# A fused attention and mixture-of-experts kernel: both halves of the small product "states times w1" put into one slot, the second half in banks of another PSUM pool

## The chip, the cores and the metric

The kernel runs as one program on one core of a Trainium2 chip. The metric is the device time of one execution in microseconds (us); lower is better. Six executions of the kernel before gave a median of 439.1 us, between 437.64 and 439.78.

The engines are named as the profile names them: PE (TensorE, the matrix engine; PEld is its loading of weights), DVE (VectorE), ACT (ScalarE), POOL (GpSimd) and SP (SyncE, which here only issues transfers). [...]

## What is computed

There are B = 8 batches with H = 8 heads, S = 512 tokens of D = 64 numbers per head, and 32 states per head. The reference, cut to what matters here:

```
scores  = scale * x @ state^T;  a  = softmax(scores)      # per batch and head
xread   = a @ state                                        # 512 rows
sread   = softmax(scale * state @ x^T) @ x                 # 32 rows
rows    = concat(xread, sread), heads side by side         # 4352 rows of 512
e       = argmax(rows @ w_gate);  g = softmax(...)[e]      # one of 8 experts for each row
out     = g * (relu(rows @ w1[e]) @ w2[e])                 # w1: 512 x 1024, w2: 1024 x 512
```

All of it is float32. The kernel uses that `xread @ w1` is `a @ (state @ w1)`: for each batch it first makes **G = states @ w1** (256 rows, that is 8 heads of 32 states, by 1024), a small product, and then multiplies the attention weights with G. G is what the change moves.

## The kernel before, in words

Each batch takes its most frequent expert. For batch b the work on PE is, in this order: G of the batch (`states_w1`, L585), the "up" product of attention weights and G with a relu (`up` L602 or `up_by_halves` L656), and the "down" product with w2 (`down` L709 or `down_by_halves` L734). Batches 0 and 1 use `down`; batches 2 to 7 use `down_by_halves`. G of batch b + 1 is made inside the down of batch b, so that the up of b + 1 can follow at once.

**`states_w1`** makes G in two halves of 512 columns. Each half takes two PSUM banks (tiles `pG`) and 8 matrix products that use only a 64 x 32 corner of the array each: 64 rows of states and 32 columns (`pg[g][ts(q, 32), :]`, q = 0..3, g = 0, 1), so the eight fill the array side by side. In the trace a float32 product is two passes, so a half is 16 instructions. The two banks of a half are then copied to the tile G by ACT.

**`down_by_halves`** computes the 512 x 1024 by 1024 x 512 product of a batch with seven half-size products in place of eight, each of 8 full-array products of 256 columns (16 passes in the trace). They stand in program order as pX, pD, pX (accumulated on the first), pY, pZ, pW, pD (accumulated). Between them lie sums: after the first pD, DVE updates the tile Sa and POOL updates the tile Ta, and both are operands of pY; after pY the same again, with Ta an operand of pW and Sa of the last pD. ACT scales pX into the rows of the result, DVE adds the other products to them, POOL issues the stores.

After product n (1 to 7) `done()` (L767) runs a **slot**: first the first part of `between_products(n)` (L1137), then one step of `slots` (`with_weights`, L1167), then the second part of `between_products(n)`. In the first part, before the change, n = 3 makes the first half of G and n = 4 the second, both in the banks of the pool `ps_t` (two banks). In the second part, n = 4 puts the four transfers of w1 for batch b + 2 on the list `lazy` (there is one w1 tile, so they wait for the last reader of the w1 before), and n = 5 lets POOL begin the sums of G and of the attention weights for the up of b + 1 (`up_sums`, L627).

A step of `slots` issues one transfer from `lazy` (SP) and then advances `work`, which from batch 2 on is **`rounds`** (L1019): three rounds for the rows of the states, sorted by expert, four experts at a time. A round transposes its rows (`ptx`), multiplies with w1 of its four experts (`pgh`, two pieces), transposes (`pth`) and multiplies with w2 (`pgy`, two pieces). A piece is 16 products, 32 passes in the trace, on a 128 x 32 part of the array each, four side by side. `rounds` yields between the pieces, so a piece falls into a slot every three to four slots: in the down of batch 3 into slot 2, of batch 4 into slot 1, of batch 5 into slot 5 (after the two `pth` of slot 4), of batch 6 into slot 3. In the down of batch 2 no piece falls into any slot. Each round's weights come through the tiles `s` (7 of 1 MB), loaded by SP from the list `need` as the pieces use them up.

The pool `ps_p` (four banks, tag "p") serves all products of up and down (`bank()`, L197); `ps_g` (two) serves the rounds and `ps_t` (two) serves G and, in batch 7, the two tiles `pE`. `evict` (L177) copies PSUM to SBUF and takes ACT and DVE in turn. The order on each engine is the order in which the program is written (`InOrder`, L40).

Of the kernel before, what the change touches and what calls it, by code (L numbers as in the profile page):

```python
# [9 lines left out]
FP32 = mybir.dt.float32  # L10
# [10 lines left out]
def kernel(  # L21
# [32 lines left out]
    pe, dve, act, gp, sp = (InOrder(e) for e in (nc.tensor, nc.vector, nc.scalar, nc.gpsimd, nc.sync))  # L54

    B, H, S, D = x.shape
# [109 lines left out]
    stG = const.tile([128, B, 4, NS], FP32)  # L166
# [27 lines left out]
    soft, rows_of = {}, {}  # L194
    G = hT = None

    def bank(name):  # L197
        return ps_p.tile([128, 512], FP32, tag="p", name=name)
# [36 lines left out]
    def turn_scores(pc, sx, i):  # L235

        dve.transpose(sx[:, i].rearrange("p b n -> p (b n)"), pc[:, i, 0:256])
# [9 lines left out]
    def exponential(sx, i):  # L247
        act.activation(sx[:, i], sx[:, i], AF.Exp, bias=0.0, scale=SCALE)
# [194 lines left out]
    def begin():  # L443

        nonlocal G, hT

# [28 lines left out]
        soft[0] = (sx,)  # L475
        G, hT = new_G(), new_hT()
        turn_scores(pc, sx, 0)
        less_max(sx, one, dve)
        exponential(sx, one)
        states_w1(G, w1s[0], stG[:, 0], (0,), cut=2)  # L480
        turn_scores(pc, sx, 1)
# [5 lines left out]
        near, far = range(NFC // 2), range(NFC // 2, NFC)  # L487
        up(G, aT[0], hT, one, fs=near)
        states_w1(G, w1s[0], stG[:, 0], (1,))
        turn_scores(pc, sx, 2)  # L490
        turn_scores(pc, sx, 3)
# [57 lines left out]
    def expert_of(table, i, engines=(SP,)):  # L549
        _, (e,) = nc.values_load_multi_w_load_instructions(  # L550
            table[0:1, i:i + 1], engines=list(engines), min_val=0, max_val=E - 1,
            skip_runtime_bounds_check_because="the table holds experts' numbers")
        return e

    w1s, w2s = {}, {}

    def w1_parts(b, e, cols=1):

        t = w1s[b] = wpool.tile([128, NDC, F], FP32, tag="w1", name="w1t")
        rows = moe_w1[ds(e, 1)].rearrange("o (c p) f -> p (o c) f", p=128)  # L560
        f = F // cols
        return [lambda k=k: sp.dma_start(out=t[:, :, ts(k, f)], in_=rows[:, :, ts(k, f)]) for k in range(cols)] if cols > 1 else \
            [lambda k=k: sp.dma_start(out=t[:, k], in_=rows[:, k]) for k in range(NDC)]

    def w2_parts(b, e):
        t = w2s[b] = wpool.tile([128, NFC, DM], FP32, tag="w2", bufs=2, name="w2t")
        rows = moe_w2[ds(e, 1)].rearrange("o (c p) f -> p (o c) f", p=128)
        return [lambda k=k: sp.dma_start(out=t[:, ts(k, 2)], in_=rows[:, ts(k, 2)]) for k in range(NFC // 2)]
# [13 lines left out]
    def new_G():  # L582
        return ffn.tile([128, 2, F], FP32, tag="G", name="G")

    def states_w1(G, w1t, st, halves=(0, 1), bank=bank, cut=1):  # L585

        for k in halves:
            pg = [bank("pG") for _ in range(2)]
            for q in range(4):
                for g in range(2):  # L590
                    pe.matmul(pg[g][ts(q, 32), :], lhsT=st[ts(g, 64), q, :],
                              rhs=w1t[ts(g, 64), q, ts(k, 512)], start=True, stop=True, skip_group_check=True)
            for c in range(cut):
                for g in range(2):
                    act.copy(G[:, g, ts(cut * k + c, 512 // cut)], pg[g][:, ts(c, 512 // cut)])
        return G

    def new_hT():

        return [ffn.tile([128, 2, S], FP32, tag="hT", bufs=NFC // 2, name="hT") for _ in range(NFC // 2)]  # L600

    def up(G, a, hT, i=ALL, insert=None, at=(1, 3, 5, 7), fs=range(NFC)):  # L602

        n = i.stop - i.start
        for f in fs:
            ph = bank("ph")[:, 0:128 * n]
            for g in range(2):
                pe.matmul(ph, lhsT=G[:, g, ts(f, 128)], rhs=a[:, i, g, :], start=(g == 0), stop=(g == 1))
            relu(hT[f // 2][:, f % 2].rearrange("p (c i t) -> p i c t", c=NC, i=4)[:, i],
                 ph.rearrange("p (i c t) -> p i c t", i=n, c=NC))  # L610
            if insert and f in at:
                next(insert, None)
        return hT
# [13 lines left out]
    def up_sums(G, a):  # L627

        Sx, Tx = new_sums("Sb"), new_sums("Tb")
        T3 = ffn.tile([128, 256], FP32, tag="T3", name="T3")  # L630
        S1, S2 = (Sx[:, ts(k, 2)].rearrange("p u t -> p (u t)") for k in range(2))
        S3 = Tx[:, 0:2].rearrange("p u t -> p (u t)")
        T1, T2, T3 = Tx[:, 2], Tx[:, 3], T3[:]

        def A(i, k):
            return G_block(G, i, k)

        def B(k, j):
            return a_block(a, k, j)

        def v(t):
            return t.rearrange("p (c i t) -> p c i t", c=2, i=4)

        gp.tensor_tensor(S1, A(1, 0), A(1, 1), ALU.add)
        gp.tensor_tensor(v(T1), B(0, 1), B(0, 0), ALU.subtract)
        gp.tensor_tensor(S2, S1, A(0, 0), ALU.subtract)
        gp.tensor_tensor(v(T2), B(1, 1), v(T1), ALU.subtract)
        gp.tensor_tensor(S3, A(0, 0), A(1, 0), ALU.subtract)
        gp.tensor_tensor(v(T3), B(1, 1), B(0, 1), ALU.subtract)

        def last():
            gp.tensor_tensor(v(T2), B(1, 0), v(T2), ALU.subtract)
            gp.tensor_tensor(S2, A(0, 1), S2, ALU.subtract)
        return S1, S2, S3, T1, T2, T3, last
# [54 lines left out]
    def down(hT, w2t, store, insert=None, between=None):  # L709
        for c in range(NC):  # L710
            py = bank("py")
            for f in range(NFC):
                pe.matmul(py[:], lhsT=hT[f // 2][:, f % 2, ts(c, 128)], rhs=w2t[:, f, :],
                          start=(f == 0), stop=(f == NFC - 1))
                if insert and f == 3:
                    next(insert, None)
            store(c, py)
            if insert:
                step = between(c)
                next(step)  # L720
                next(insert, None)
                next(step)
# [123 lines left out]
    def store_batch(b):  # L846
        rows = out[ds(b * SO, S)].rearrange("(p c) f -> p c f", c=NC)

        def store(c, py):
            y = ffn.tile([128, DM], FP32, tag="y", bufs=YB, name="y")  # L850
            act.activation(y[:], py[:], AF.Copy, scale=gw[:, NC * b + c, :])
            no_dep(act.dma_start(out=rows[:, c], in_=y[:]))
        return store
# [76 lines left out]
    late = {}  # L930
# [191 lines left out]
    def batch(b):  # L1122

        nonlocal G, hT

        def between(c):
            nonlocal G
            if c == 1 and b:
                G = states_w1(new_G(), w1s[b + 1], stG[:, b + 1])
            yield  # L1130
            if c == 2 and not b:
                G = states_w1(new_G(), w1s[b + 1], stG[:, b + 1])
            if c == 1 and 0 < b < B - 2:
                lazy.extend(w1_parts(b + 2, expert_of(eb, b + 2)))
            yield

        def between_products(n):  # L1137
            nonlocal G
            if n in (3, 4) and b + 1 < B:
                if n == 3:  # L1140
                    G = new_G()
                states_w1(G, w1s[b + 1], stG[:, b + 1], (n - 3,),
                          lambda name: late["ps_t"].tile([128, 512], FP32, tag="t", bufs=2, name=name))
            yield
            if n == 4 and b + 2 < B:
                lazy.extend(w1_parts(b + 2, expert_of(eb, b + 2)))
            if n == 5 and b + 1 < B:
                sums_of[b + 1] = up_sums(G, aT[b + 1])
            yield

        if b < NE:
            down(hT, w2s[b], store_batch(b), slots, between)
        else:
            last = down_by_halves(b, hT, w2s[b], slots, between_products)
        if 0 < b < B - 2:
            lazy.extend(w2_parts(b + 2, expert_of(eb, b + 2)))
        if b + 1 in sums_of:
            hT = up_by_halves(G, aT[b + 1], sums_of[b + 1], new_hT(), slots)
        elif b + 1 < B:
            hT = up(G, aT[b + 1], new_hT(), insert=slots, at=(1, 3, 5, 7) if b + 1 < NE else (1, 3, 4, 5, 6, 7))  # L1160
        if b == B - 1:
            return last
        if b == 0:
            e2 = expert_of(eb, 2)
            lazy.extend(w1_parts(2, e2) + w2_parts(2, e2))
# [12 lines left out]
    for b in range(B):  # L1178
        last = batch(b)
# [116 lines left out]
```

## Time and profile before

| what | value |
|---|---|
| median of 6 executions | 439.1 us (437.64 to 439.78) |
| the profiled execution | 438.35 us; its span, from first to last instruction, 434.3 us |
| PE busy | 426.1 us of the span (98%) |
| DVE, ACT, POOL busy | 220.3, 128.9 and 153.3 us |
| granted TensorE clock | 1.000 over the whole span |
| transfers | 110.04 MB, mean 253 GB/s |
| G in the downs of batches 2 to 6 | 10 halves of 1.02 us each in the chain of work that ended last |

The profile's page gives busy time of each engine, the span in 40 slices, the chain of work that ended last (followed back from the last instruction), and groups of instructions by operation and tile. The chain in order of time lists pieces as start, length and tile; lengths in it are from the start of one piece to the start of the next on the chain, so two pieces that differ by what precedes them differ in length. The timeline lists instructions by engine with the idle time before them. All operations are recorded through one helper, so every line is L48, and tiles tell them apart.

The downs with `down_by_halves` begin at 163.85 (batch 2), 206.88 (3), 253.98 (4), 304.42 (5), 351.48 (6) and 397.95 us (7).

### The profile page before, as it was taken

The numbers are of one execution on the slowest core, as the hardware profiler recorded it, in microseconds if no ns is written. First come the engines' busy times: TensorE is split into PE (matmuls) and PEld (weight loads), VectorE is DVE, ScalarE is ACT, GpSimd is POOL, SyncE is SP. The second block draws the span as 40 slices with busy tenths as digits, with TensorE's granted clock in tenths as the row PEclk, the third lists the DMA queues.
The fourth block names the chain that finished last, engine by engine and source line by source line (L and its number), as shares of the span: only waits on it lengthen the run. The fifth ranks groups of instructions, "written<-read, shape, count | busy, mean of one in ns | idle before, by whom it ended". The sixth has DMA issues, their size and how long they took to land.

```text
span 434.3 us, 10177 instructions
## 1 busy us (share of the span) xinstructions
PE 426.1 (98%) x3927; PEld 289.7 (67%) x3927; DVE 220.3 (51%) x473; ACT 128.9 (30%) x297; POOL 153.3 (35%) x143
## 2 busy tenths in 40 slices
PE   7899999999999999999999999999999999999996
PEld 7676555555545558686668667776867685768665
DVE  5668967587686547434424251624442370527142
ACT  1455134552451532213221241013240242015100
POOL 2010231233222512473327424634336253644231
PEclk9999999999999999999999999999999999999999
DMA  5991559653685454899999799689947998875312
GB/s 146 338 339 45 190 195 334 192 209 127 203 309 171 158 173 123 298 345 399 339 379 398 249 333 391 257 288 396 386 142 258 374 385 286 312 273 187 97 35 73
DMA packets 64513, 110.04 MB, mean 253 GB/s; under 512 B 12943, under 2 KB 22415, under 8 KB 64464
## 3 DMA queue, kind: packets, MB, share of 16 engines
q1 hardware_dynamic: 60240, 99.99, 67.1%
q0 software_dynamic: 2240, 7.08, 4.3%
q10 hardware_dynamic: 1984, 2.31, 1.5%
q8 instruction: 32, 0.52, 0.5%
q14 instruction: 17, 0.14, 0.1%
HBM read 94.15 MB, written 14.95 MB: 251 GB/s over the span
## 4 chain that ended last, share of the span: by engine, by line
PE 95%; DVE 2%; DMA 1%; ACT 0%; issue 0%; ACTq 0%; POOL 0%; DVEq 0%
PE ph L48 23%; PE py L48 13%; PE pX L48 10%; PE pD L48 8%; PE pY L48 5%; PE pZ L48 5%; PE pgh L48 5%; PE pgy L48 5%; PE pW L48 5%; PE pc L48 4%; PE pG L48 3%; PE pw L48 2%; PE pt L48 2%; PE pE L48 2%; DMA wg<-in_moe_w_gate_dram 1%; PE pl L48 1%
## 5 line engine op out<-in xcount | busy, mean ns | idle before, releaser
L48 PE MATMUL py<-w2t,hT 128*128 128x512 f32 x128 | 59.1, 604 | 0.0
L48 DVE TENSOR_TENSOR hT<-ph,hT 128x512 f32<-128x512 f32 x50 | 34.6, 692 | 40.7 <-PE ph L48 40.7
L48 POOL TENSOR_TENSOR Ta<-w2t,Ta 128x1024 f32<-128x1024 f32 x12 | 30.6, 2548 | 46.6 <-PE pY L48 19.9
L48 PE MATMUL pX<-w2t,hT 128*128 128x256 f32 x192 | 43.7, 381 | 0.0
L48 PEld LDWEIGHTS py<-w2t,hT 128*128 128x128 f32 x128 | 23.0, 189 | 26.3 <-issue 25.3
L48 PEld LDWEIGHTS pX<-w2t,hT 128*128 128x128 f32 x192 | 36.2, 190 | 6.4 <-issue 1.7
L48 ACT ACTIVATE hT<-ph 128x512 f32<-128x512 f32 (+2 forms) x50 | 22.7, 461 | 40.2 <-PE ph L48 40.2
L48 PE MATMUL ph<-aTl,G 128*128 128x256 f32 (+1 forms) x112 | 33.8, 444 | 0.0
L48 DVE SCALAR_TENSOR_TENSOR yh<-pY,gw,yh 128x256 f32<-128x256 f32 x22 | 9.2, 478 | 44.3 <-PE pY L48 37.7
L48 PE MATMUL ph<-aTe,G 128*128 128x128 f32 (+2 forms) x128 | 30.4, 388 | 0.6 <-DVE aTe L48 0.4
L48 ACT ACTIVATE yh<-pX,gw 128x256 f32<-128x256 f32 x34 | 13.7, 473 | 52.6 <-PE pX L48 52.6
L48 POOL DMA_DIRECT2D out_dram<-yh x23 | 16.8, 730 | 34.2 <-DVE yh L48 17.6
L48 ACT ACTIVATE hT<-hT 128x512 f32<-128x512 f32 x30 | 18.9, 630 | 30.7 <-DVE hT L48 30.7
L48 PEld LDWEIGHTS ph<-aTl,G 128*128 128x128 f32 x112 | 20.6, 190 | 9.6 <-issue 7.7
L48 POOL TENSOR_TENSOR sx<-sx,mx 128x1024 f32<-128x1024 f32 x6 | 11.5, 1913 | 38.5 <-DVE mx L48 38.5
L48 PEld LDWEIGHTS ph<-aTe,G 128*128 128x128 f32 x128 | 18.8, 191 | 9.3 <-issue 6.5
L48 ACT COPY G<-pG 128x512 f32<-128x512 f32 (+1 forms) x34 | 17.1, 568 | 24.3 <-PE pG L48 24.3
L48 PE MATMUL pY<-Ta,Sa 128*128 128x256 f32 x96 | 22.2, 384 | 0.0
L48 ACT COPY hT<-ph 128x512 f32<-128x512 f32 x10 | 5.9, 585 | 55.1 <-issue 43.1
L48 PE MATMUL pZ<-Tb,Sb 128*128 128x256 f32 x96 | 22.1, 383 | 0.0
L48 PEld LDWEIGHTS pY<-Ta,Sa 128*128 128x128 f32 x96 | 17.8, 190 | 6.4 <-issue 3.4
L48 POOL TENSOR_TENSOR Tb<-w2t 128x1024 f32<-128x1024 f32 x6 | 14.2, 2367 | 22.2 <-issue 22.2
(184 smaller groups left out, 737.6 us busy)
## 6 DMA issues: line engine op xcount, KB each, us to landing
s<-in_moe_w_dram SPq DMA_DIRECT2D x192, 256.0 KB, 6.0
w2t<-in_moe_w_dram SPq DMA_DIRECT2D x32, 512.0 KB, 6.8
w1t<-in_moe_w_dram SPq DMA_DIRECT2D x28, 512.0 KB, 6.1
x_nat<-in_x_dram SPq DMA_DIRECT2D x16, 512.0 KB, 6.4
out_dram<-yh POOLq DMA_DIRECT2D x23, 256.0 KB, 5.4
at_dram<-aTl SPq DMA_DIRECT2D x6, 512.0 KB, 3.5
w1t<-in_moe_w_dram SPq DMA_DIRECT2D x2, 1024.0 KB
out_dram<-y ACTq DMA_DIRECT2D x8, 256.0 KB, 4.9
```

The source lines that it names most:

```text
L48: ins = getattr(self.engine, name)(*args, **kw)
```

## The change

For batches 3 to 7 (made in the downs of batches 2 to 6) both halves of G are made in one slot: slot 3, 2, 1, 5 and 3 in the downs of batches 2, 3, 4, 5 and 6. The first half uses the two banks of `ps_t` as before, the second two of the four banks of `ps_p`. The four copies to G alternate between ACT and DVE (`evict`) where all four were ACT's. The list of w1 transfers for batch b + 2 is put on `lazy` in the same slot instead of slot 4. The start of `up_sums` stays in slot 5.

```
-    def states_w1(G, w1t, st, halves=(0, 1), bank=bank, cut=1):
+    def states_w1(G, w1t, st, halves=(0, 1), bank=bank, cut=1, copy=None):
...
-                    act.copy(G[:, g, ts(cut * k + c, 512 // cut)], pg[g][:, ts(c, 512 // cut)])
+                    (copy or act.copy)(G[:, g, ts(cut * k + c, 512 // cut)], pg[g][:, ts(c, 512 // cut)])
...
+        at = {3: 2, 4: 1, 5: 5}.get(b, 3)
+
+        def late_bank(name):
+            return late["ps_t"].tile([128, 512], FP32, tag="t", bufs=2, name=name)
+
         def between_products(n):
             nonlocal G
-            if n in (3, 4) and b + 1 < B:
-                if n == 3:
-                    G = new_G()
-                states_w1(G, w1s[b + 1], stG[:, b + 1], (n - 3,),
-                          lambda name: late["ps_t"].tile([128, 512], FP32, tag="t", bufs=2, name=name))
-            yield
-            if n == 4 and b + 2 < B:
+            if n == at and b + 1 < B:
+                G = states_w1(new_G(), w1s[b + 1], stG[:, b + 1], (0,), late_bank, copy=evict)
+                states_w1(G, w1s[b + 1], stG[:, b + 1], (1,), copy=evict)
+            yield
+            if n == at and b + 2 < B:
                 lazy.extend(w1_parts(b + 2, expert_of(eb, b + 2)))
             if n == 5 and b + 1 < B:
                 sums_of[b + 1] = up_sums(G, aT[b + 1])
```

The order of the instructions on PE in these downs, read from both programs (P is a piece of a round, G a half of G):

```
down of   before                              after
batch 2   pX pD pX G pY G pZ pW pD            pX pD pX GG pY pZ pW pD
batch 3   pX pD P pX G pY G pZ pW pD          pX pD GG P pX pY pZ pW pD
batch 4   pX P pD pX G pY G pZ ptx pW P pD    pX GG P pD pX pY pZ ptx pW P pD
batch 5   pX pD pX G pY G pth pZ P pW pD      pX pD pX pY pth pZ GG P pW pD
batch 6   pX pD ptx pX G P pY G pZ pW pD P    pX pD ptx pX GG P pY pZ pW pD P
```

## The prediction, made before the result was known

> **What bounds the kernel now.** I read the page first, then who waits on PE, then the chain of work in order of time.
>
> ```profile
> span 434.3 us, 10177 instructions
> PE 426.1 (98%) x3927; PEld 289.7 (67%) x3927; DVE 220.3 (51%) x473; ACT 128.9 (30%) x297; POOL 153.3 (35%) x143
> PE 95%; DVE 2%; DMA 1%; ACT 0%; issue 0%; ACTq 0%; POOL 0%; DVEq 0%
> ```
>
> PE is busy for 98% of the span, and 95% of the chain that ended last is PE. Busy time per stretch says it more sharply: from 163 to 398 us, the downs and ups that the change touches, PE is busy 235.0 of 235.0 us. In the waits of PE the only one of any size on a transfer of w1 is 0.9 us, and that is the first G of the kernel. So nothing stands ahead of PE there: the time is the sum of PE's pieces, and a change counts for what it takes from that sum or for a wait that it brings. The pieces, from the chain in order of time:
>
> ```profile
> 122.94 1.88 PE pG L48 x32
> ...
> 210.33 3.45 PE pD L48 x16
> 213.78 3.57 PE pgh L48 x32
> 217.35 3.65 PE pX L48 x16
> 221.00 1.02 PE pG L48 x16
> 222.02 3.65 PE pY L48 x16
> 225.67 1.02 PE pG L48 x16
> 226.69 3.65 PE pZ L48 x16
> 230.34 3.45 PE pW L48 x16
> ...
> 237.25 0.87 PE pth L48 x8
> ...
> 319.45 1.02 PE pG L48 x16
> 320.47 1.02 PE pth L48 x8
> 321.49 3.46 PE pZ L48 x16
> ...
> 362.28 1.02 PE pG L48 x16
> 363.30 3.57 PE pgh L48 x32
> 366.87 3.65 PE pY L48 x16
> ```
>
> What to see: the same 16 passes of a full-array product take 3.45 us after another full-array product (pD, pW) and 3.65 us after a narrow one (pX after `pgh`, pY and pZ after `pG`). So **coming back from a narrow product costs 0.20 us**. `pth` shows it too: 0.87 us after a full product, 1.02 after `pG`; the pZ behind it is then 3.46. **Entering** costs as well: a half of G takes 1.02 us, both halves at a stretch (batches 0 and 1 make them so) 1.88, so a half is (1.88 - 1.02) = 0.86 us of work and 0.16 of entry. And a piece of a round takes 3.57 us whether `pG` (at 363.30) or a full product (at 213.78) stands before it: between two kinds of narrow product the entry stays due, but no return is paid.
>
> **The change on PE.** Only the order moves; the count of products is the same. Down by down, from the rows above:
>
> - batch 2: before G, pY, G, pZ = 1.02 + 3.67 + 1.02 + 3.65 = 9.36 (its pY is 3.67). After GG, pY, pZ = 1.88 + 3.65 + 3.45 = 8.98. Gain 0.38.
> - batch 3: before P, pX, G, pY, G, pZ = 3.57 + 3.65 + 1.02 + 3.65 + 1.02 + 3.65 = 16.56. After GG, P, pX, pY, pZ = 1.88 + 3.57 + 3.65 + 3.45 + 3.45 = 16.00. Gain 0.56: one entry and two returns.
> - batch 4: the same pieces, with P before pD: gain 0.56.
> - batch 5: before G, pY, G, `pth`, pZ, P = 1.02 + 3.65 + 1.02 + 1.02 + 3.46 + 3.57 = 13.74. After pY, `pth`, pZ, GG, P = 3.45 + 0.87 + 3.46 + 1.88 + 3.57 = 13.23. Gain 0.51.
> - batch 6: its first half already stands before a piece. Before G, P, pY, G, pZ = 1.02 + 3.57 + 3.65 + 1.02 + 3.65 = 12.91. After GG, P, pY, pZ = 1.88 + 3.57 + 3.65 + 3.45 = 12.55. Gain 0.36.
>
> Sum: 0.38 + 0.56 + 0.56 + 0.51 + 0.36 = **2.37 us**. A GG over banks of two pools is not in the trace; its bounds are 1.72 (2 x 0.86, no entry) and 2.04 (2 x 1.02), that is 0.8 us to either side over five of them. I take 1.88, the nearest row.
>
> [...]
>
> **What the change could cost, and what hides it.**
>
> *Copies of G.* Twenty copies were ACT's; ten go to DVE. Rows: `G<-pG` on ACT 589 ns, `shT<-pth` on DVE (same shape, also from PSUM) 684 ns. DVE gains 10 x 0.684 = 6.8 us in a stretch where it is busy 96 of 235 us. On DVE they wait for `pG`, with work queued behind them: in the downs of batches 2, 3 and 6 the additions of pY, in 4 the scaling of a round's result and then Sa for pY, in 5 the additions of pW. Each of these waits for a PE product that ends later than GG, so nothing is held. G itself is needed by `up_sums`, which still begins in slot 5. In batch 5 that is the tightest: GG ends at about 323.0 on the new clock, the copies about 1.3 us later, POOL's four sums for the first dependent product (1.28 + 0.73 + 1.28 + 0.73 = 4.0) at about 328.4, and that product would start at about 335. ACT loses 10 x 0.589 = 5.9 us, which brings nothing, since no PE product waits for ACT there. Cost 0.
>
> *Banks.* While GG is in two banks of `ps_p`, pX and pD may hold the other two. In batch 4 the second half takes banks whose last readers were DVE's additions of the up before, over at about 255 when GG starts at 256.5; in batch 5 it takes those of pX and pY, whose reader on DVE ends 1.7 us after pY, some 3.5 us before. pY then takes pX's bank or one that G has left, whose copy is under way while the product before pY runs (or, in batch 2, pX's, read by ACT in 0.84 us while GG runs for 1.88). Cost 0.
>
> *Sums that lose their cover.* pY needs Ta from POOL, started at the end of pD; pW needs Ta again, started at the end of pY. Until now a G stood in between as well. These two lines of POOL's timeline (start, length; pD ended at 311.33, pY at 319.45) give the margins:
>
> ```profile
> 311.47 2.79 POOL L48 TENSOR_TENSOR Ta<-w2t,Ta 128x1024 f32<-128x1024 f32 x1 [6.27 <-PE pD L48]
> 319.61 2.37 POOL L48 TENSOR_TENSOR Ta<-w2t,Ta 128x1024 f32<-128x1024 f32 x1 [2.93 <-PE pY L48]
> ```
>
> Ta is ready 0.14 + 2.79 = 2.93 us after pD and 0.16 + 2.37 = 2.53 after pY. With one product of 3.45 us in between, the margin is 0.52 us for pY (downs of 4 and 5 lose G there) and 0.92 for pW (2, 3, 6; 4 has `ptx` too). Tight, but no wait: cost 0; its bounds are 0 and what the rival below gives.
>
> *Transfers.* In the downs of 2, 3, 4 the w1 list goes to SP one to three slots earlier, in 5 one slot later. SP's queue runs in order, so what counts is what stands around it. w1 for batch 4 is issued up to 197.92 us, behind the 20 transfers of `s`, in both orders; the longest time to landing of an `s` transfer was 9.5 us, so it is there by 207.4. Its readers move from 221.0 to about 213.4: margin 6.0 us. w1 for batch 5 was issued up to 233.46 and is read at 256.5 in place of 268.1; w1 for batch 7 comes with the three parts that SP issued at 338 to 340 before, and is read at about 360. None of the `s` transfers falls behind something that waits longer than before. Cost 0.
>
> **Sum.** Span 434.3 - 2.37 = 431.9; with the 4.05 us that lie around the span, 438.35 - 2.37 = 436.0 for the profiled execution. That execution is 0.75 us under the median of those shown; on the median's scale 439.1 - 2.4 = **436.7 us**. A difference under 0.3% (1.3 us) can't be told from no change.
>
> **Rivals.**
>
> 1. *The two halves don't run together.* If the second half, in other banks and with waits of its own, pays its entry again, GG is 2.04, not 1.88: 5 x 0.16 = 0.8 us less, 437.5. For it: in batches 0 and 1 all four banks were of one pool. Against it: a wait that is long fulfilled cost nothing visible elsewhere in the chain. Still faster.
> 2. *The sums become the wait.* If Ta comes later than it did, pY or pW waits. In batch 2 Ta was held behind POOL's transfers and ended at 175.23, 4.37 us after pD. If pY in 4 and 5 met that, it would wait 4.37 - 3.45 = 0.92 us each, 1.8 in all: 439.1 - 2.4 + 1.8 = 438.5, within 0.3%. The round's store on POOL in batch 4 (1.06 us, at 262.19) lies in front of Ta there, but ends 1.4 us before pD does. An entry and return price that is not saved at all would end here too.
> 3. *The earlier G waits for w1* (the other side). Place: GG in the down of batch 3, 7.6 us earlier than its first half was. It decides once w1 lands after 213.4, that is 15.5 us after its issue in place of at most 9.5; each us beyond is a us of PE. To be slower by 0.3% it has to be 3.7 us beyond: 440.4 at least, I price it 441. For it: DMA is 93 to 94% busy in the stretches of batches 3 and 4. Against it: the margin of 6.0 us.
>
> **Chances.** My sum 0.63; rival 1 0.16; rival 2 (with the switch price not saved) 0.14; rival 3 0.07. Faster by over 0.3%: the first two, 0.79 with 437.5 safely under 437.8; same 0.14; slower 0.07. The range reaches from 435.2 (the sum, with the run's spread of some 0.3% below) to 438.7, past rival 2, and leaves out rival 3 and a little at each end.
>
> **What would show it.** Right: `pG` in five pieces of 1.88 us in the chain; pY in batches 3, 4, 5 and pZ everywhere at 3.45; `pth` in batch 5 at 0.87; PE busy without gaps; the down of batch 7 beginning near 395.6 in place of 397.95. Wrong: pieces of 2.0 us (rival 1); pY or pW over 3.5 with idle PE released by POOL Ta (rival 2); PE `pG` waiting for the w1 transfer (rival 3).

## The result, and the profile after

The changed kernel takes **437.73 us** (median of 23 executions, 436.02 to 439.39); the kernel before, measured over 48 executions by then, 438.83 us (437.51 to 440.0). The ratio is 0.9975, with a 95% interval of [0.9966, 0.9984]. So 1.1 us were gained where 2.4 were forecast: the direction and the range were right, the gain was less than half of the forecast, and under the 0.3% that was set as the bound of "faster". This section finds that the gain inside the kernel came in full and that 1.1 us were lost *outside the span*, in executions in which transfers of the kind "instruction", taken here for program code, still run after the last instruction.

The profiled execution of the changed kernel took 436.1 us, of which the span is 431.5 (before: 438.35 and 434.3). From its page, the span, the busy time of the engines and the chain by engine:

```profile
span 431.5 us, 10177 instructions
PE 422.5 (98%) x3927; PEld 290.1 (67%) x3927; DVE 226.4 (52%) x483; ACT 123.9 (29%) x287; POOL 153.0 (35%) x143
PE 94%; DMA 2%; DVE 2%; issue 0%; ACT 0%; ACTq 0%; POOL 0%; SPq 0%; DVEq 0%
```

PE is still the bound. Ten instructions went from ACT (297 to 287) to DVE (473 to 483), whose busy time grew by 6.1 us, and this lengthened nothing. (Each copies a PSUM tile of 128 x 512 float32, `pG`, to the tile G in SBUF; in the down of batch 2 one took 0.586 us on ACT and 0.692 on DVE.) PE's first 163 us vary from one execution to the next: the first pX began at 163.34 to 164.37 us in five profiled executions with this order on PE. To leave that out, I compare a **section**: from the start of the first pX (down of batch 2) to the end of the last pE. Before it is 427.08 + 3.47 - 163.85 = 266.70 us, after 424.22 + 3.47 - 163.34 = **264.35 us**. That is 2.35 us less, against 2.37 forecast.

The chain of work of the changed kernel in order of time (start, length, engine, tile) shows the pieces that answer to those of before, for the downs of batches 2, 3, 5 and 6 and the start of the down of batch 7:

```profile
173.81 1.88 PE pG L48 x32
175.69 3.65 PE pY L48 x16
179.34 3.45 PE pZ L48 x16
...
212.90 1.88 PE pG L48 x32
214.78 3.57 PE pgh L48 x32
218.35 3.65 PE pX L48 x16
222.00 3.45 PE pY L48 x16
225.45 3.45 PE pZ L48 x16
...
316.24 0.87 PE pth L48 x8
317.11 3.46 PE pZ L48 x16
320.56 1.88 PE pG L48 x32
322.44 3.57 PE pgy L48 x32
...
359.77 1.88 PE pG L48 x32
361.65 3.57 PE pgh L48 x32
365.22 3.65 PE pY L48 x16
368.87 3.45 PE pZ L48 x16
...
395.09 3.45 PE pX L48 x16
```

What to see: `pG` is one piece of 32 passes and 1.88 us, in banks of two pools as in banks of one. Each product that no longer follows a narrow product is at 3.45 in place of 3.65 (pZ everywhere, pY in batch 3), `pth` at 0.87 in place of 1.02. Next to a piece of a round, GG takes its entry and leaves the return to the piece. No product of this stretch waits. The down of batch 7 begins 395.09 - 163.34 = 231.75 us after the first pX; before it was 397.95 - 163.85 = 234.10.

POOL's timeline of the changed kernel, in the down of batch 4, answers to the sum that lost its cover:

```profile
265.25 2.78 POOL L48 TENSOR_TENSOR Ta<-w2t,Ta 128x1024 f32<-128x1024 f32 x1 [1.57 <-PE pD L48]
```

Ta is ready at 268.03, pX ends and pY begins at 268.55: the margin of 0.52 us that the forecast gave, to the hundredth.

**Where the rest went.** The time of an execution is its span and what lies around it. The kernel before has 4.05 us around its span in the profiled execution, and medians of 4.02 to 4.17 in the four sets of executions that ran beside the experiments (70 in all). The changed kernel has 4.6 us in the profiled execution and a median of **5.19** over 25 (4.52 and more in every one). That is 1.1 us more; 2.35 - 1.1 = 1.2 is about the gain that was measured. The spans alone, over the same 25 executions, have a median of 432.5 us, against 434.5 to 434.8 in the four sets of the kernel before: inside the span the gain of some 2 us is there over all executions. The trace records transfers after the last instruction too. Those of the kind "instruction" (16 KB each on queue q8, 8 KB on q14), called transfers of code here after that name, lie like this, in us from the end of the last instruction (start to end):

```
                  q8 in all   q8, late         q14, late
before            32          none             2.06 to 2.50
changed           33          3.20 to 4.89     four, from 2.76-2.95 to 3.15-3.31
```

The 33rd transfer of code is there only in the changed kernel, and ends later than everything else in its trace. That the execution ends with such a late transfer, and what brings it, is the theory which the later experiments test.

### The profile page after: what moved, and what is told of

Same layout as the page of the kernel before. It is cut to its first block, busy times and chain, and to the rows that moved or that the text cites. A ratio compares the mean times of both kernels' runs of the same rounds, so it can differ in the third digit from the quotient of the medians.

```text
span 431.5 us, 10177 instructions
## 1 busy us (share of the span) xinstructions
PE 422.5 (98%) x3927; PEld 290.1 (67%) x3927; DVE 226.4 (52%) x483; ACT 123.9 (29%) x287; POOL 153.0 (35%) x143
## 4 chain that ended last, share of the span: by engine, by line
PE 94%; DMA 2%; DVE 2%; issue 0%; ACT 0%; ACTq 0%; POOL 0%; SPq 0%; DVEq 0%
PE ph L48 23%; PE py L48 13%; PE pX L48 10%; PE pD L48 8%; PE pgh L48 5%; PE pgy L48 5%; PE pW L48 5%; PE pY L48 5%; PE pZ L48 5%; PE pG L48 4%; PE pc L48 3%; PE pw L48 2%; PE pt L48 2%; PE pE L48 2%; DMA w1t<-in_moe_w_dram 1%; DMA wg<-in_moe_w_gate_dram 1%
## 5 line engine op out<-in xcount | busy, mean ns | idle before, releaser
L48 PE MATMUL pW<-Ta,hT 128*128 128x256 f32 x96 | 21.9, 381 | 0.0
L48 PE MATMUL pgh<-s,sxT 128*32 128x512 f32 x192 | 21.8, 595 | 0.0
L48 PE MATMUL pgy<-s,shT 128*32 128x512 f32 x192 | 21.8, 595 | 0.0
```

The costliest lines, as they stand in the source:

```text
L48: ins = getattr(self.engine, name)(*args, **kw)
```

## The experiments

Times are medians; each ratio is to the kernel before on the same chip, with its 95% interval. "Section" is the stretch defined above, "around" the median of time minus span over the kernel's executions.

| run | time, us | ratio | section, us | around, us | 33rd code transfer on q8 |
|---|---|---|---|---|---|
| changed kernel again | 437.38 | 0.9963 [0.9950, 0.9976] | 264.35 | 5.47 | yes |
| two slots, second half in `ps_p` | 442.46 | 1.0073 [1.0057, 1.0089] | 270.53 | 4.17 | no |
| slot 3 in every down | 437.0 | 0.9952 [0.9934, 0.9970] | 264.94 | 4.18 | no |
| four quarters | 442.1 | 1.0074 [1.0055, 1.0093] | 269.83 | 4.68 | inside the span |
| two slots, both in `ps_t` | 438.75 | 1.0003 [0.9992, 1.0013] | 266.69 | 4.21 | no |
| one slot, both in `ps_t` | 444.55 | 1.0125 [1.0107, 1.0144] | 270.65 | 5.71 | yes |
| changed, one PE product less at the start | 438.02 | 0.9975 [0.9966, 0.9985] | 264.35 | 5.44 | yes |
| before, two PE products more | 438.83 | 0.9997 [0.9986, 1.0008] | 266.68 | 4.14 | no |
| changed, three more on POOL, at its start | 436.26 | 0.9956 [0.9941, 0.9971] | 264.35 | 4.25 | no |
| changed, three more on SP | 437.42 | 0.9971 [0.9957, 0.9985] | 264.34 | 5.07 | yes |
| before, three fewer on POOL | 439.98 | 1.0041 [1.0026, 1.0056] | 266.69 | 5.51 | yes |
| changed, three more on POOL, at its end | 436.49 | 0.9947 [0.9931, 0.9963] | 264.34 | 4.20 | no |

### First set: the price of a change, the banks and the copies

My theory after the result was that the price per change of product holds in full and that the rest is lost outside the section. The rival was that the new banks or the copies on DVE cost some 1.2 us within the kernel.

**The changed kernel again**, beside the others and without an edit.

> The changed kernel once more, against the kernel before on the same chip. Theory A (price of entering and leaving a narrow product): the part of the chain from the down of batch 2 to the last PE product is 2.35 us shorter, as in the first profile after (264.37 against 266.72 us), and the time is 2.4 us less, unless the stretch before 163 us or what lies around the span differs between the two kernels; then the span shows where. Theory B (a cost that the profiled execution doesn't show: the copies on DVE or the banks of the other pool give back half): the time is 1.1 us less again, and the spans differ by 1.1 too.

Section 264.35 us once more, 5.47 us around. The medians of the spans differ by 2.7 us (432.1 against 434.8), those of the times by 1.4, so theory B falls. The loss belongs to the program, not to one set of executions.

**Two slots.** The halves stay in slots 3 and 4, as before, with the changed kernel's banks and copies:

```
+            if n == 3 and b + 1 < B:
+                G = states_w1(new_G(), w1s[b + 1], stG[:, b + 1], (0,), late_bank, copy=evict)
+            if n == 4 and b + 1 < B:
+                states_w1(G, w1s[b + 1], stG[:, b + 1], (1,), copy=evict)
```

> Only the banks and the alternating copies of the change, with the two halves of G left in slots 3 and 4 and the w1 list where it was. Theory A: PE's pieces are those of before (G 1.02, the product behind it 3.65), so the time is that of before within 0.4 us. Theory B: this part alone costs about 1.2 us, 440.0 where before has 438.8.

Both expectations missed: the section grew by 3.83 us. The waits of PE (operation, what it waited for, us in total, times, longest) and the chain of this kernel say why:

```profile
PE pZ L48 <- DVE yh L48: 3.5, 4, 1.2
```

```profile
174.60 1.02 PE pG L48 x16
175.62 3.67 PE pY L48 x16
179.32 0.42 issue
179.84 0.29 issue
180.14 1.27 DVE yh L48 x3
181.45 3.72 PE pZ L48 x16
```

pY ends at 179.3 and pZ begins at 181.45. In between the second half runs (it lies under "issue" and DVE: the chain leaves PE here) and DVE's addition of pY ends. pD, pY and the second half's two tiles fill the four banks of the pool, and so pZ gets pY's own bank and waits for its reader, in four of five downs. In the fifth `pth` stands in between. In the changed kernel the same banks cost nothing because GG runs where the two banks are free. So "banks cost 0" is true of the place, not of the banks.

**Slot 3 in every down.** One line of the changed kernel:

```
-        at = {3: 2, 4: 1, 5: 5}.get(b, 3)
+        at = 3
```

> Both halves in one slot as in the change, but in slot 3 of every down, so that only in batch 6 a piece of a round stands behind them. Theory A: one entry and one return less in each down: 0.38 + 0.36 + 0.36 + 0.31 + 0.36 = 1.8 us less than before, 0.6 more than the changed kernel. Theory B: 1.8 less 1.2, so 0.6 us less than before.

The section is 264.94 us, 1.76 less than before. Standing GG beside a piece of a round is thus worth the other 0.59. Though its section is longer, its whole time is not: its median is 0.4 us under that of the changed kernel beside it (437.0 and 437.38; the intervals of the two ratios overlap). It has no 33rd transfer, and 4.18 us around.

**Four quarters.** In the kernel before, G is made in four groups of 256 columns, in slots 2 to 5, in the banks of `ps_t`, copied by ACT:

```
+        for q in range(4):
+            for g in range(2):
+                pe.matmul(pg[g][ts(q, 32), 0:256], lhsT=st[ts(g, 64), q, :],
+                          rhs=w1t[ts(g, 64), q, ts(k, 256)], start=True, stop=True, skip_group_check=True)
...
-            if n in (3, 4) and b + 1 < B:
+            if n in (2, 3, 4, 5) and b + 1 < B:
```

> The kernel before with each half of G cut once more: quarters of 256 columns in slots 2, 3, 4 and 5, banks and copies as before. Work on PE is equal, the entries and returns of G double. Theory A: by the rows of before a quarter is 0.43 of work and 0.16 of entry, 0.20 for the return: 0.72, 0.52, 0.72, 0.52 and 0.67 more in the downs of batches 2 to 6, 3.2 us more than before. If the price is in what the profile models and not in the time, the time stays.

The section grew by 3.13 us and the time by 3.3, so the price is not only in what the profile models. The chain of this kernel in the down of batch 2:

```profile
174.34 0.59 PE pG L48 x16
174.93 3.65 PE pY L48 x16
178.58 0.59 PE pG L48 x16
179.17 3.65 PE pZ L48 x16
```

A quarter is 0.43 us of work (half of 0.86) and 0.16 of entry, and each product behind one pays 0.20. The two prices hold with twice as many changes as with fewer; the rival that a change of kind is not what is saved falls.

### Second set: banks alone, copies alone, and code

Two kernels part the banks from the copies. Two more test the first form of the code theory, which the expectations call theory C: that a different number of instructions on **PE** puts the end of its program differently against the pieces in which code is loaded. (PE's program has six instructions more in the changed kernel, all of them waits: the traces hold 106 semaphore instructions on PE against 100.)

**Two slots, both halves in `ps_t`**, with copies alternating between ACT and DVE: the two-slot kernel with `late_bank` for the second half as well.

> As e2 (halves in slots 3 and 4, alternating copies), but both halves in the banks of ps_t as before: the alternating copies alone. If e2's loss is the wait of pZ for a bank that DVE still reads (4 waits, 3.5 us, in its profile), it goes here and the time is that of before within 0.4 us. If the copies on DVE are at fault, 1 us or more stays.

Section 266.69 us, against 266.70 before: the copies cost nothing. And since only the second half's banks set it apart from the two-slot kernel above, the 3.84 us between them are the wait for pY's bank.

**One slot, both halves in `ps_t`**: the changed kernel with its second half in the two banks of the first.

```
-                states_w1(G, w1s[b + 1], stG[:, b + 1], (1,), copy=evict)
+                states_w1(G, w1s[b + 1], stG[:, b + 1], (1,), late_bank, copy=evict)
```

> The changed kernel with both halves in the two banks of ps_t. The second half has to wait for the copies of the first: about 0.2 us to their start and 0.59 or 0.68 of copy, while PE has nothing to do. Theory A: some 0.9 us in each of five downs, 4.5 in all, against the gain of 2.35: 2.2 us slower than before, 441. Its PE program is 4 instructions shorter than that of before and SP's and POOL's are as short as in the changed kernel, so by theory C there is no transfer of code at the end.

Of this kernel the waits of PE and the chain in the down of batch 2:

```profile
PE pG L48 <- ACT G L48: 4.5, 5, 1.2
```

```profile
174.56 1.16 PE pG L48 x16
175.72 0.57 ACT G L48
176.34 1.24 PE pG L48 x16
177.57 3.65 PE pY L48 x16
```

From 174.56 to 177.57 it is 3.01 us for what takes 1.88 in two pools: the second half waits for the copies of the first, and both halves are longer themselves (1.16 and 1.24 us). In all the section is 6.30 us longer than the changed kernel's. The waits are what was expected (4.5 us); the rest is mostly in the longer halves. The second pool is what makes one slot possible.

**Changed, one PE product less; before, two more.** The products that keep PE busy at the start (`keep_warm`) on `idle`, from three to two, and from three to five:

```
-        keep_warm(3)
+        keep_warm(2)
```

> The changed kernel with one warming product less at its very start (keep_warm(3) to keep_warm(2)), where PE waits for the first loads anyway: PE's program is 4 instructions shorter, nothing after 6 us is touched. Theory C (a piece of PE's code is fetched at the end of the program: in both profiles of the changed kernel a 33rd transfer of 16 KB on the instruction queue q8 starts 3.2 us after the last instruction, and the time lies 4.6 and 5.7 us over the span; the kernel before, e2 and e3 have 32 such transfers, none at the end, and lie 4.05 over their spans; PE has 6 instructions more than before in the changed kernel, 4 in e2, 3 in e3): the 33rd transfer goes, the time lies about 4.05 over the span, and it is 436.4 us, 2.4 less than before. Rival D (the lost microsecond is a wait in executions without the profiler): the time stays at 437.4.

> The kernel before with two warming products more at its start (8 PE instructions more). Theory C: the 33rd transfer appears at the end, the time lies 4.6 to 5.7 us over the span, and the kernel is about 1 us slower than before, 439.8. Rival D: the time is that of before within 0.3 us.

Neither moved: 438.02 us with the 33rd transfer still there, 438.83 without it. The kernel with one slot and both halves in `ps_t` has the transfer too, against its expectation, with a PE program four instructions shorter than that of the kernel before. The theory falls in its PE form. What the programs with the 33rd transfer after the end have in common is elsewhere: **POOL's program has 319 instructions and SP's 992**, against 322 and 994 or 995 in all others (counted in the compiled programs; of these the traces hold those that ran, 250 and 983 against 253 and 985 or 986). The missing three are waits on semaphores (in the traces 89 against 92 on POOL, 100 against 103 on SP), which the page doesn't count (POOL shows x143 before and after). It is the slots that take them away: the kernel with slot 3 in every down has 322 and 995.

### Third set: POOL's program or SP's

**Three more on POOL, at its start** (changed kernel; the result is written once more and is the same):

```
+    for _ in range(3):
+        gp.iota(jio[:], pattern=[[1, NG]], base=0, channel_multiplier=0,
+                       allow_small_or_imprecise_dtypes=True)
```

> The changed kernel with three iota instructions more on POOL at its start, so that POOL has 322 instructions as in the kernel before, and SP stays at 992. Section from the first pX to the end of pE: 264.35 us by every theory. Theory C-POOL (the transfers after the last instruction depend on the length of POOL's program): the late transfers go, 4.05 to 4.2 us lie around the span, time 264.35 + 172.1 = 436.4. Theory C-SP (they depend on the length of SP's program): the late transfers stay, time 437.4 to 438.0. Neither: as C-SP.

**Three more on SP** (changed kernel; three transfers are made in two halves each):

```
+        for h in range(2 if b in (4, 5, 6) else 1):
+            w = 512 if b in (4, 5, 6) else 1024
+            sp.dma_start(out=at_dram[b][:, ts(h, w)], in_=rows[:, ts(h, w)])
```

> The changed kernel with three transfers more on SP's queue (the reads that are kept in the downs of batches 4, 5 and 6 are made in two halves each), so that SP has 995 instructions as in the kernel before, and POOL stays at 319. Section 264.35 us by every theory. C-SP: the late transfers go, time 436.4. C-POOL: they stay, 437.4 to 438.0. If both this one and the one with three instructions more on POOL keep them, neither length alone decides.

**Three fewer on POOL** (kernel before; three such fills):

```
-    gp.memset(ones_b[:], 1.0)
+    dve.memset(ones_b[:], 1.0)
```

> The kernel before with three fills at its start made by DVE in place of POOL, so that POOL has 319 instructions as in the changed kernel, SP stays at 995. Section 266.7 us by every theory. C-POOL: the late transfers appear, time 266.7 + 173.4 = 440.1, slower than before by 1.3. C-SP: no late transfers, 438.8, no difference.

POOL decides, in both directions. (DVE, which takes the three fills, is not what decides: the two-slot kernel has ten copies more on DVE than the kernel before, and no such transfer.) The first has the page's span of the changed kernel and yet is 1.16 us faster than the second, on the same chip; the second's line stands below the first's:

```profile
span 431.5 us, 10180 instructions
```

```profile
span 431.6 us, 10178 instructions
```

The last transfers of code, in us from the last instruction's end:

```
                             q8 in all   q8, late        q14, late
changed, POOL + 3            32          none            2.06 to 2.56, 4.30 to 4.79
changed, SP + 3              33          3.12 to 4.93    four, from 2.76-3.27 to 3.26-3.58
before, POOL - 3             33          3.10 to 4.84    four, from 2.76-3.22 to 3.22-3.52
```

The kernel before, with three fills moved from POOL to DVE, got slower by 0.41% with an unchanged section, and the transfer appeared. The changed kernel, given three idle instructions, lost the transfer and gained what was missing.

**Three more on POOL, at its end**: the same three `gp.iota`, now behind `last()` at the end of the program (with what orders them POOL has 324 instructions). It tells the program's length from what POOL does or loads first.

> The changed kernel with three iota instructions more on POOL behind its last work, not at its start (with what orders them POOL has 324 instructions). Section 264.35 us. Theory C-POOL, by length: the late transfers go, 4.05 to 4.2 us around the span, 436.3. Rival, that it was the three instructions' place at the start that mattered (what POOL loads or does first): the late transfers stay, 437.4 to 437.7.

436.49 us, no 33rd transfer, 4.20 us around. The place at the start is not what matters.

Over all profiled executions, the end of the last transfer of code, in us after the last instruction, stands beside the time around the span of the same execution. The last one is the 33rd on q8 in the changed kernel, in "SP + 3" and in "POOL - 3"; in all other rows it is one of 8 KB on q14.

```
                                        last code transfer ends   around the span
changed                                 4.89                      4.6
changed again                           6.01                      5.7
changed, one PE product less            5.73                      5.44
one slot, both in ps_t                  5.77                      5.55
four quarters                           4.92                      4.67
changed, POOL + 3 at the start          4.79                      4.5
changed, POOL + 3 at the end            4.39                      4.1
changed, SP + 3                         4.93                      5.0
before, POOL - 3                        4.84                      4.9
before and the four others              2.4 to 2.6                4.05 to 4.2
```

Where the last transfer ends after 4.3 us, the time around the span is within some 0.3 us of that end; where none does, some 4.1 us remain.

The two kernels with three more on POOL also have the lowest medians: 436.26 and 436.49 us, below the kernel before (438.57 and 438.6 beside them) and below the changed one.

## Why the prediction was right, and where its size was wrong

- **The time is the sum of PE's pieces: right.** The changed stretch has no wait of PE, and section and sum agree to 0.02 us.
- **Return 0.20, entry 0.16 us: right.** The pieces came out at 1.88, 3.45, 3.57 and 0.87 as listed. Fewer changes (slot 3 in every down, -1.76) and more (quarters, +3.13) follow the same two prices.
- **Rival 1, a second entry for the second half: did not happen.** Five pieces of 1.88. Where both halves share two banks the second is longer (1.24 us in the down of batch 2), but there a wait for the copy goes with it.
- **Copies at nothing: right**, shown alone by the two-slot kernel in `ps_t` (266.69 against 266.70 us).
- **Banks at nothing: right for this place**, and the argument by readers that are done in time was needed: in slots 3 and 4 the same banks cost 3.84 us.
- **Sums at nothing, rival 2: did not happen.** The margin was 0.52 us as worked out, and nothing exceeded it.
- **Transfers at nothing, rival 3: did not happen.** PE's only wait for w1 is still the first G of the kernel.
- **"With the 4.05 us that lie around the span": this step failed.** It took a row that the change doesn't touch as constant. It is 5.2 us in the changed kernel, as a median. The forecast on the median's scale, 439.1 - 2.4 = 436.7, is met by the changed kernel with three more instructions on POOL (436.26 and 436.49), and missed by the changed kernel itself (437.73). The term was mis-sized by 5.19 - 4.05 = 1.1 us, about what the forecast is off by (437.73 - 436.7 = 1.0; in gains, 2.4 - 1.1 = 1.3).

What stays open is why a further load goes with a POOL program that is *shorter* by three. The transfers on q8 are of 16,384 bytes each, those of code at the end on q14 of 8,192. No run here moved POOL's length in steps to find the edge: 322 and 324 instructions are on one side, 319 on the other. Nor is it shown that the further load is POOL's code. From 163 to 398 us q8 makes 11 transfers in the kernel before, while PE and PEld record 2711 instructions, 246 for each; the kernel of quarters, with 320 more of them, makes one more transfer inside its span. From these figures I estimate that q8 brings PE's code; no run shows whose code it is. Together with the four on q14 the 33rd makes five late transfers, as many as there are engines, so POOL's length may decide whether all engines load once more; that is a guess, and no run tests it.

That the transfer itself is what delays the end, and not something else that happens with it, rests on its company in every run (the ends above; in medians 5.07 to 5.71 us around with a 33rd transfer after the end, 4.02 to 4.25 with none), not on a run that holds back the transfer alone.

## What to carry to other kernels

When PE runs without gaps, list its pieces with what stands before each: what a reordering gains is the number of changes between kinds of products times the prices read from the chain. Here such sums came out to within 0.1 us on the section (2.37 forecast and 2.35 measured, 1.8 and 1.76, 3.2 and 3.13). A free bank is a statement about a place in the order: name the last reader of each bank that a moved product gets, and its time. Gains of a microsecond must be compared with what lies around the span, in several executions: an edit that only moves waits can change the length of an engine's program (here POOL's from 322 to 319 instructions), and with it what is loaded after the last instruction (here a 33rd transfer, and 1.1 us).

## What the runs showed of the hardware that was not expected

- Code is still being transferred after the last instruction, and the time goes with it: with a 33rd transfer of 16 KB on q8, from 3.1 to 4.9 us after the end, 5.07 to 5.71 us lie around the span, without it 4.02 to 4.25. Three instructions more or less on POOL switch it on and off; a product less or two more on PE, or three instructions more on SP, don't. The kernel of quarters, with 33 such transfers inside its span and a late one of 8 KB on q14, lies between, at 4.68.
- A half of G that waits for its own banks costs more than the wait: 3.01 us for the pair in the down of batch 2 in place of 1.88, where the copy that it waits for takes 0.586 us on ACT and 0.691 on DVE.
